# Blocks of keys handled whole: four score products, then one product with V, and the maxima tasks taken from buffers of their own

## The chip, the cores and the metric

The kernel runs on one core of one Trainium2 chip. The metric is the device time of one execution in microseconds, lower is better. The core has five engines with a queue each: PE (matrix products, from SBUF into PSUM), DVE (vector), ACT (scalar, exponentials), POOL and SP, which issues most of the DMAs here. PSUM has eight banks of 128 x 512 float32. PEld stands for the loading of PE's weights.

## The reference, cut to what matters

Two attentions over the same 2048 tokens (512 wide, 32 heads of 16) are mixed by a gate:

```
a = A(x): causal softmax attention inside 4 segments of 512, plus a linear-attention memory of earlier segments
b = B(x): qkv = x @ wqkv;  p = softmax(q k^T / 4) over all 2048 keys;  o = p v;  o @ wo
out = g * a + (1 - g) * b,     g = sigmoid(x . gate_w)
```

B is the larger part: 32 heads x 2048 x 2048 scores, all exponentiated.

## The kernel before, in words

**Projection stage** (lines 766 to 944). The images of q and k (float16, high and low halves) and of v are computed with products of twelve matmuls each (`qk_job`, `v_job`; line 311 and line 285) and stored in DRAM. A loop over 16 blocks `blk` does this for A with its memory, and takes jobs for B from a list `fill`. Between the jobs `spill()` issues pairs of maxima tasks.

**Rounds** (lines 1050 to 1085). A round `k` (32 of them) handles one unit of B and one of A; a unit is four heads (a quad) and 512 queries. In this text a *period* is one block `it` of 128 keys of a B unit, 16 per round, and the *A stretch* is what follows them in the round.

- In a period, `t_group` makes the scores of B transposed (keys on partitions): two groups, `n` even and odd, of two heads each. Heads 0 and 2 use rows 0 to 63 of PE, heads 1 and 3 rows 64 to 127, so that two products on different halves run side by side. The banks come from `T3` = `tb0`, `tb1`, `mb`. ACT exponentiates each bank into one of two buffers `PTILE`.
- `pv` multiplies the exponentials of the period before with V, four heads on four column strips, into the bank `pvb`. It is called for 256 queries after each of the two groups.
- **Maxima tasks**: the exponent of a later round needs row maxima. A task `s_b` multiplies 128 queries by 512 keys for two heads (two matmuls, line 535, into a pair of banks `sbk`) and DVE reduces the 128 x 1024 result to 128 x 2 (line 537). A unit has 32 tasks, 1024 in all. `spread` plans two per period for the next rounds' units; each stands *between* the two score products of a group (`between`), so that each of its halves runs beside one of them. `sbk` has two pairs, used in turn. The tasks read the same `QB` and `KB` buffers (three of each) as the score products.
- The A stretch has five groups of A (`t_group`, `pv`) and the six masked maxima reductions of the next A unit (`s_a`, lines 513 to 524).
- `m_chain` turns the maxima of the next units into two rows, `m_rows` puts them into the operands, `fin_copy`, `fin_load`, `fin_rec`, `fin_bc`, `fin_norm` normalise, `out_rows` (from round 9 on, a half of a 128-row block per round) multiplies by the output weights, split by rows into two banks.

The order of the work on every engine is the order in which the code is written; a queue runs in that order and waits at its head.

Of the kernel before, what the change touches and what calls it, by code (L numbers as in the profile page):

```python
# [7 lines left out]
FT = mybir.dt.float32  # L8
# [12 lines left out]
SEQ = 2048  # L21
DM = 512
C = 512
# [7 lines left out]
EARLY = 6  # L31
S_FIRST = 10
S_LAST = 10
OMI = 14
SPILLS = 64
# [3 lines left out]
def gated_mix_kernel(ctx, tc, xt, wq, wk, wv, wo, beta, wqkv, wob, gate_w, out):  # L39
# [10 lines left out]
    QB = [P.tile([128, 2, C], HF, name=f"qb{s}") for s in range(3)]  # L50
# [18 lines left out]
    KB = [P.tile([128, 2, SEQ], HF, name=f"kb{s}") for s in range(3)]  # L69
    KBF = [t.rearrange("p a t -> p (a t)").bitcast(FT).rearrange("p (k t) -> p k t", k=4) for t in KB]  # L70
# [377 lines left out]
    def load_qk(dst, kd, w, qd, c):  # L448
# [4 lines left out]
        for d0, r0, n in ((0, 0, 16), (16, 0, 32)) if w else ((0, 0, 32), (32, 16, 18)):  # L453
            for j in range(2):
                nc.sync.dma_start(dst[64 * j + d0:64 * j + d0 + n], v[qd % 2, j, r0:r0 + n, :, cs])
# [5 lines left out]
    def q_of(u):  # L461
        return QA[u % 2] if u < 32 else QB[u % 3]

    def k_of(u, p):
        return KA[u % 2][:, p] if u < 32 else KB[(u - 32) % 3][:, p]
# [9 lines left out]
    def load_kb(k, c=None):  # L475
        dst = KB[k % 3] if c is None else KB[k % 3][:, :, c * C:(c + 1) * C]
        load_qk(dst, "B", 1, k % 8, c)
# [48 lines left out]
    MXB = {}  # L526

    def s_b(u, i, p, kc):
        kd, qd, c = UN[u]
        if u not in MXB:  # L530
            MXB[u] = W.tile([128, 2, 2, 4, 4], FT, name="mxb")
        b = rot("s", SBK)
        for j in (1, 0):
            r = slice(64 * j, 64 * j + 64)
            nc.tensor.matmul(b[:, j], q_of(u)[r, p, i * 128:(i + 1) * 128],  # L535
                             k_of(u, p)[r, kc * C:(kc + 1) * C], start=True, stop=True)
        nc.vector.tensor_reduce(MXB[u][:, :, p, i, kc], b, axis=AX.X, op=OP.max)  # L537
# [3 lines left out]
    def m_chain(k):  # L541
# [3 lines left out]
        if k < 32:  # L545
            nc.vector.tensor_reduce(mx[:, 1], MXB.pop(32 + k).rearrange("q j p i c -> q (j p) i c"), axis=AX.X,
                                    op=OP.max)
        else:
            nc.vector.memset(mx[:, 1], 0.0)
# [33 lines left out]
    def t_group(u, n, banks, between=()):  # L583
# [5 lines left out]
        for it, hs in (((n // 2, (n % 2 * 2, n % 2 * 2 + 1)),) if kd == "B" else GA[n]):  # L589
# [3 lines left out]
            for j, h in enumerate(hs):  # L593
# [6 lines left out]
                PT[u, it, h] = PTILE[pn % 2][:, 2 + j if (kd, it) == ("A", 2) else h][:, c0:c0 + w]  # L600
            c0 += w
        for j in range(2):
            pt = PTILE[pn % 2][:, 2 + j if (kd, n) == ("A", 4) else hs[j]]
# [82 lines left out]
    def out_mm(c, t, a):  # L686

        b = misc()
        for n, (oi, wi, g) in enumerate([(oi, wi, g) for oi, wi in TERMS for g in range(4)]):
            nc.tensor.matmul(b, (AT["oh"], AT["ol"])[oi][:, g, a], (AT["wh"], AT["wl"])[wi][:, g, a],  # L690
                             start=n == 0, stop=n == 11)
# [7 lines left out]

    def out_rows(c, t, a, inner):  # L700
        b = [misc(), rot("s", SBK)[:, 0]]
        for n, (oi, wi, g) in enumerate([(oi, wi, g) for oi, wi in TERMS for g in range(4)]):
            for j in range(2):
                r = slice(64 * j, 64 * j + 64)
                nc.tensor.matmul(b[j], (AT["oh"], AT["ol"])[oi][r, g, a], (AT["wh"], AT["wl"])[wi][r, g, a],  # L705
                                 start=n == 0, stop=n == 11)
            if n == 2:
                for f in inner:
                    f()
                rot("s", SBK)  # L710
        if a == 0:
            AT["y"] = [AT["L"].tile([128, DM], FT, name=n) for n in ("yo", "yp")]
            nc.scalar.activation(AT["y"][0], b[0], AF.Copy)
            nc.vector.tensor_copy(AT["y"][1], b[1])
        else:
            tt = 4 * c + t
            y0, y1 = AT["y"]
            y2 = AT["L"].tile([128, DM], FT, name="yq")
            nc.scalar.activation(y2, b[0], AF.Copy)
            nc.vector.tensor_tensor(y1, b[1], y1, op=OP.add)  # L720
            nc.gpsimd.tensor_tensor(y0, y0, y2, op=OP.add)
            nc.gpsimd.tensor_tensor(y0, y0, y1, op=OP.add)
            nc.sync.dma_start(outr[tt * 128:(tt + 1) * 128, :], y0)
# [36 lines left out]
    ST_B = [(i, p, kc) for i in range(4) for p in range(2) for kc in range(4)]  # L760
    ST_A = [(0, None), (2, 0), (2, 1), (3, 0), (3, 1), (1, None)]

    def s_tasks(u):
        return [todo(s_a, u, *t) for t in ST_A] if u < 32 else [todo(s_b, u, *t) for t in ST_B]
# [21 lines left out]
    ax = [todo(set_aux, t[:, p], int(n < 3)) for n, t in enumerate(QB + KB[:1]) for p in range(2)]  # L786
    ax = [todo(set_steps, t[:, p], a) for a, ts in enumerate((KA, QA)) for t in ts for p in range(2)] + ax
    for tt in range(NT):
# [29 lines left out]
        if ax:  # L818
            ax.pop(0)()
    for n in range(8):  # L820
        w, c = divmod(n, 4)
        qk_job(0, "B", 0, w, c)
        if n < 4:
            split_wv(n)
# [8 lines left out]
    first = s_tasks(32) + s_tasks(0)  # L833
    st33 = [todo(s_b, 33, *t) for t in sorted(ST_B, key=lambda t: t[2])]
    early = st33[:EARLY]
# [7 lines left out]
    def spill():  # L843
        nonlocal quota
        quota += rate
        if quota >= 2:
            quota -= 2
            for _ in range(2):
                (first or early).pop(0)()

    S0 = [b[:, 0] for b in SBK]
    CUM = (2, 4, 6, 9, 11, 13, 16, 18, 20, 22, 24, 27, 29, 32, 34, 36)
    for blk in range(16):
        g, c = divmod(blk, 4)
        pg, pc = divmod(blk - 1, 4)
        if blk == 4:
            mode["misc"] = TB + [MB, PVB]
        rate = len(ST_A + ST_B) / SPILLS if 4 <= blk < 14 else 0
        if blk == 14:
            for p in range(2):  # L860
                set_aux(KB[1][:, p], 0, nc.sync)
            load_kb(1, 0)
# [9 lines left out]
        if blk == 2:  # L872
# [13 lines left out]
        if blk == 4:  # L886
            load_q(33)
# [19 lines left out]
        for n in range(3):  # L907
            for f in mt[n]:
                f()
            if blk == 14 and n == 2:  # L910
                quota = EARLY
# [4 lines left out]
            if blk == 14:  # L916
                load_kb(1, 1 + n)
            if nf == 35:
                mode["misc"] = [MB, PVB, TB[1]]
# [11 lines left out]
        if blk == 13:  # L931
            for f in first:
                f()
            first, quota = [], 0
        if 0 < c < NC4 - 1:
            mem_upd(g, c)
        if blk == 14:
            spill()
        if blk == 15:
            for f in early:  # L940
                f()
# [3 lines left out]


    def late():
# [9 lines left out]
        for p in range(2):  # L957
            set_aux(KB[2][:, p], 0)
# [4 lines left out]
    NG = 2 * NT + 5  # L963

    def pvs(k, n):

        ua, ub = k, 32 + k
        if n == 0:
            if k:
                pv(ua - 1, 2)  # L970
                fin_copy(ua - 1)
        elif k == 31 and n < 2 * NT:
            if n % 2 and n > 1:
                pv(ub, n // 2 - 1)
        elif 2 <= n < 2 * NT + 2:
            pv(ub, n // 2 - 1, n % 2 * 256, n % 2 * 256 + 256)
            if n == 2 * NT + 1:
                fin_copy(ub)
        elif n > 2 * NT + 1:
            m = n - 2 * NT - 2  # L980
            if m < 2:
                pv(ua, 0, 256 * m, 256 * m + 256)
            else:
                pv(ua, 1)
                pv(ua, 3)

    def extras(k):

        pre, post = {}, {}
        if not k:  # L990
            for n in range(4):
                pre[2 * n] = [fill[n - 4]]
        post[2 * S_LAST + 4] = [todo(m_rows, k + 1)]
        for n, at in [(k - 9, 1)] + [(23, 2 * OMI)] * (k == 31):
            if n >= 0:
                rows = (n // 8, n // 2 % 4, n % 2)
                pre[at] = [todo(out_rows, *rows, plan.pop((k, at))) if k < 31 else todo(out_mm, *rows)]
        return pre, post

    def beside(k, it):  # L1000

        for f, it0, u in ((fin_load, NT + 1, 32 + k), (fin_rec, 5, 31 + k), (fin_bc, 6, 31 + k),
                          (fin_load, 1, k - 1), (fin_rec, 6, k - 1), (fin_bc, S_LAST + 2, k - 1)):
# [30 lines left out]
    plan = {}  # L1034

    def spread(tasks, gs):
        for n, p in enumerate(gs):
            plan.setdefault(p, []).extend(tasks[len(tasks) * n // len(gs):len(tasks) * (n + 1) // len(gs)])

    for k in range(31):  # L1040
        if k:
            spread([todo(s_b, 33 + k, *t) for t in (sorted(ST_B, key=lambda t: t[2]) if k == 1 else ST_B)],
                   [(k - 1, n) for n in range(2 * S_FIRST, 2 * NT)] + [(k, n) for n in range(2 * S_LAST)])
        else:
            spread(st33[EARLY:], sorted([(0, n) for n in range(2 * S_LAST)] + [(0, 2 * n) for n in range(4)]))
        for n, t in enumerate(ST_A):
            plan.setdefault((k, 2 * NT + n - (n > 2)), []).append(todo(s_a, k + 1, *t))

    ex = [extras(k) for k in range(32)]
    for k in range(32):  # L1050
        ua, ub = k, 32 + k
# [89 lines left out]
```

## Time and profile before

| what | value |
|---|---|
| median of 3 runs | 1846.73 us (1845.93 to 1847.3) |
| profiled execution | 1849.68 us, span 1848.0 us, granted clock 0.997 |
| PE busy | 1807.7 us, 98% of the span |
| DVE busy | 1591.2 us, 86% |
| ACT busy | 1432.4 us, 78% |
| POOL busy | 339.3 us, 18% |
| DMA | 158.92 MB, mean 86 GB/s |

The profiled execution is 3 us above the median. A row of the timeline gives the start, the duration, the engine, the line, the operation and the operands; rows of one kind that follow each other are merged (x8). Matmuls are pipelined, so the distance between starts says how long one holds the engine, and its duration how long it takes to be done. On PE a float32 product with V shows as two records.

### The profile page before, as it was taken

How to read it: one execution, taken by the hardware profiler on the slowest of the kernel's cores; microseconds unless marked ns; L12 is line 12 of the kernel's file. 1: busy time of each engine (PE TensorE's matmuls, PEld its weight loads, DVE VectorE, ACT ScalarE, POOL GpSimd, SP SyncE). 2: the span in 40 equal slices, each digit the busy share in tenths (PEclk: the TensorE clock that was granted, in tenths of full speed). 3: DMA queues.
4: the chain of work that ended last, by engine and by line, in shares of the span. 5: the costliest groups of instructions: out<-in, count | busy, mean ns of one | idle time of the engine just before them, and what ended most of it. 6: DMA issues, size and time to landing. Idle time of an engine off the chain costs nothing.

```text
span 1848.0 us, 44286 instructions
## 1 busy us (share of the span) xinstructions
PE 1807.7 (98%) x17781; PEld 730.0 (40%) x17781; DVE 1591.2 (86%) x1772; ACT 1432.4 (78%) x2709; POOL 339.3 (18%) x691
## 2 busy tenths in 40 slices
PE   8999999899999999999999999999999999999998
PEld 6677777532222222333333333333333333333325
DVE  6334786699999999999999999999999999999942
ACT  4233333388989999989898989898989898989894
POOL 6100000101212010212121212121212121212122
PEclk9999999999999999999999999999999999999999
DMA  7554534332323222323232323232323232323111
GB/s 229 92 141 141 148 99 106 87 96 68 97 74 93 61 80 64 79 68 85 67 85 67 85 68 85 67 86 67 85 68 85 67 85 69 87 69 87 47 39 61
DMA packets 162482, 158.92 MB, mean 86 GB/s; under 512 B 40140, under 2 KB 126620, under 8 KB 162276
## 3 DMA queue, kind: packets, MB, share of 16 engines
q1 hardware_dynamic: 158692, 149.29, 29.1%
q0 software_dynamic: 3296, 6.27, 1.8%
q8 instruction: 140, 2.29, 0.5%
q14 instruction: 66, 0.54, 0.1%
q10 hardware_dynamic: 288, 0.52, 0.1%
HBM read 103.38 MB, written 50.86 MB: 83 GB/s over the span
## 4 chain that ended last, share of the span: by engine, by line
PE 80%; DVE 13%; ACT 4%; issue 2%; DMA 1%; SPq 0%; ACTq 0%; DVEq 0%; POOLq 0%
PE pvb L620 29%; PE tb L598 12%; DVE mxb L537 10%; PE sbk L535 10%; PE mb L598 6%; PE tb L311 3%; ACT raw L604 3%; PE pvb L311 2%; PE tb L705 2%; PE tb L285 2%; PE sbk L513 2%; PE sbk L285 2%; PE mb L705 1%; PE mb L311 1%; PE sbk L311 1%
## 5 line engine op out<-in xcount | busy, mean ns | idle before, releaser
L537 DVE TENSOR_REDUCE mxb<-sbk 128x2 f32<-128x1024 f32 x1024 | 1173.7, 1221 | 24.7 <-PE sbk L535 13.1
L604 ACT ACTIVATE raw<-tb 128x512 f32<-128x512 f32 x1557 | 884.5, 600 | 64.5 <-PE tb L598 30.9
L620 PE MATMUL pvb<-raw,vb 128*17 128x256 f32 (+1 forms) x8072 | 645.2, 388 | 0.0
L535 PE MATMUL sbk<-kb,qb 64*128 64x512 f16 x2048 | 552.8, 378 | 9.3 <-DVE mxb L537 8.3
L604 ACT ACTIVATE raw<-mb 128x512 f32<-128x512 f32 x780 | 468.2, 600 | 31.5 <-PE mb L598 14.4
L598 PE MATMUL tb<-qb,kb 64*128 64x512 f16 x1343 | 467.0, 381 | 1.2 <-ACT raw L604 0.8
L598 PEld LDWEIGHTS <-kb 64*128 64x128 f16 x2048 | 143.6, 93 | 414.4 <-issue 409.3
L620 PEld LDWEIGHTS pvb<-raw,vb 128*17 128x17 f32 x8072 | 138.0, 95 | 403.3 <-issue 393.8
L598 PE MATMUL mb<-qb,kb 64*128 64x512 f16 x678 | 258.2, 381 | 1.1 <-DVE st L326 1.0
L607 POOL TENSOR_SCALAR_AFFINE_SELECT raw<-raw 128x256 f32<-128x256 f32 (+1 forms) x320 | 115.3, 361 | 326.6 <-ACT raw L604 318.3
L535 PEld LDWEIGHTS <-qb 64*128 64x128 f16 x2048 | 137.3, 93 | 43.4 <-issue 33.5
L521 DVE TENSOR_REDUCE mx<-sbk 128x2 f32<-128x1024 f32 (+1 forms) x128 | 133.9, 1088 | 7.0 <-PE sbk L517 5.9
L620 PE MATMUL pvb<-raw,va 128*17 128x256 f32 (+2 forms) x1280 | 103.2, 383 | 3.8 <-ACT pvs L629 1.1
L664 POOL TENSOR_TENSOR o<-o,d 128x512 f32<-128x512 f32 x31 | 39.5, 1274 | 216.5 <-DMA d<-rd 175.9
L523 DVE TENSOR_REDUCE mx<-sbk 128x4 f32<-128x512 f32 x64 | 61.3, 958 | 12.4 <-PE sbk L517 12.4
L513 PE MATMUL sbk<-ka,qa 64*128 64x512 f16 (+3 forms) x512 | 70.5, 296 | 0.0
L598 PE MATMUL tb<-qa,ka 64*128 64x384 f16 (+3 forms) x340 | 61.7, 303 | 0.0
L652 POOL TENSOR_TENSOR rec<-rec,grow 128x16 f32<-128x16 f32 x24 | 5.3, 221 | 275.9 <-DVE rec L644 275.9
L323 ACT ACTIVATE st<-tb,rng 128x512 f16<-128x512 f32 x21 | 14.4, 687 | 53.0 <-PE tb L311 19.8
L517 PE MATMUL sbk<-cmask,crows 64*128 64x64 bf16 x1024 | 52.7, 189 | 0.0
L517 PEld LDWEIGHTS <-crows 64*128 64x128 bf16 x1024 | 46.4, 94 | 13.7
L445 POOL TENSOR_TENSOR mst<-mtmp,mst 128x136 f32<-128x136 f32 x8 | 3.6, 452 | 257.8 <-DVE mtmp L444 257.8
(330 smaller groups left out, 1732.1 us busy)
## 6 DMA issues: line engine op xcount, KB each, us to landing
vb<-vdB SPq DMA_DIRECT2D x16, 1088.0 KB
pd<-pvs SPq DMA_DIRECT2D x64, 256.0 KB
kb<-dB SPq DMA_DIRECT2D x60, 256.0 KB
dB<-st SPq DMA_DIRECT2D x64, 128.0 KB
dA<-st SPq DMA_DIRECT2D x64, 128.0 KB
o<-pd SPq DMA_DIRECT2D x64, 128.0 KB
d<-rd SPq DMA_DIRECT2D x63, 128.0 KB
kb<-dB SPq DMA_DIRECT2D x60, 128.0 KB
```

The costliest lines, as they stand in the source:

```text
L285: nc.tensor.matmul(b, (XH, XL)[xi][c][:, n % 4, tl * 128:(tl + 1) * 128], WV[wi][:, n % 4, :], start=n == 0, stop=n == 11)
L311: nc.tensor.matmul(b, WS[ws][w][wi][:, k, :], (XH, XL)[xi][c][:, k, :], start=n == 0, stop=n == 11)
L513: nc.tensor.matmul(b[:, j, c0:c0 + n], q_of(u)[r, p, i * 128:(i + 1) * 128], k_of(u, p)[r, :n], start=True, stop=False)
L517: nc.tensor.matmul(b[:, j, c0 + n - 128 + w.start:c0 + n - 128 + w.stop], crows[r, n2 - 1], cmask[r, n2 - 1, w], start=False, stop=n2 == 2)
L521: nc.vector.tensor_reduce(m[:, :, p, i], b[:, :, :n], axis=AX.X, op=OP.max)
L523: nc.vector.tensor_reduce(m[:, :, :, i], b.rearrange("q j (p k) -> q j p k", p=2)[:, :, :, :n], axis=AX.X, op=OP.max)
L535: nc.tensor.matmul(b[:, j], q_of(u)[r, p, i * 128:(i + 1) * 128], k_of(u, p)[r, kc * C:(kc + 1) * C], start=True, stop=True)
L537: nc.vector.tensor_reduce(MXB[u][:, :, p, i, kc], b, axis=AX.X, op=OP.max)
L598: nc.tensor.matmul(bs[j][:, c0:c0 + w], k_of(u, h // 2)[r, 128 * it:128 * it + 128], q_of(u)[r, h // 2, q0:], start=True, stop=True)
L604: nc.scalar.activation(pt, bs[j], AF.Exp, scale=AT["esc", kd, qd // 2])
L607: nc.gpsimd.affine_select(out=m, in_=m, pattern=[[1, 128]] if n < 2 else [[0, 2], [1, 128]], compare_op=OP.is_ge, fill=0.0, base=0, channe ...
L620: nc.tensor.matmul(PVB[32 * h:32 * h + E + 1, q0 + lo:q0 + hi], vt[:, it, 4 * q + h, :], pt[:, lo:hi], start=it == 0 and lo == 0, stop=it ...
```

## The change

In words:

- A period issues all four score products of a block of keys, into four banks `ET` = `tb0`, `tb1` and the two halves of the *second* pair `sbk1`; then one product with V over all 512 queries (`b_group`, `pv`). The order of the heads alternates with the half task (below).
- A period carries one and a half maxima tasks instead of two: a full one in the *first* pair `sbk0`, and one half of a second task in the bank `mb`, whose other half goes into the next period (`half_task`). In the A stretch some five more full tasks stand (`extra`).
- The tasks have operand buffers of their own (`QM`, `KM`, two each, loaded by `fetch`) and take units in the order `ORD`; their results lie in eight places of `MXB`. `AHEAD` = 160 tasks (before: 32, and six of the next unit) are issued in the projection stage, in pairs after the jobs from block 2 on, before round 0.
- `out_rows` is gone; `out_mm` makes a whole product into `mb` in the A stretch, with one task inside. `QB` and `KB` have two buffers instead of three, and SP loads them at period 2 of the round before.

```diff
-EARLY = 6
-S_FIRST = 10
-S_LAST = 10
-OMI = 14
-SPILLS = 64
+AHEAD = 160
+SPILLS = 96
+CHAIN_AT = 10
+ROWS_AT = 12
...
-    QB = [P.tile([128, 2, C], HF, name=f"qb{s}") for s in range(3)]
+    QB = [P.tile([128, 2, C], HF, name=f"qb{s}") for s in range(2)]
+    QM = [P.tile([128, 2, C], HF, name=f"qm{s}") for s in range(2)]
+    MXB = P.tile([128, 8, 2, 2, 4, 4], FT, name="mxb")
...
-    KB = [P.tile([128, 2, SEQ], HF, name=f"kb{s}") for s in range(3)]
+    KB = [P.tile([128, 2, SEQ], HF, name=f"kb{s}") for s in range(2)]
+    KM = [P.tile([128, 2, SEQ], HF, name=f"km{s}") for s in range(2)]
...
+    ORD = [0, 8, 1, 9, 2, 3, 4, 5, 6, 7] + list(range(10, 32))
+    TASKS = [(n, i, p, kc) for n in range(32) for i in range(4) for p in range(2) for kc in range(4)]
...
+    def s_red(b, t, js):
+        n, i, p, kc = t
+        m = MXB[:, place[n][1], :, p, i, kc]
+        if len(js) == 2:
+            nc.vector.tensor_reduce(m, b, axis=AX.X, op=OP.max)
+        else:
+            nc.vector.tensor_reduce(m[:, js[0]:js[0] + 1], b, axis=AX.X, op=OP.max)
+        if (i, p, kc) == (0, 1, 0):
+            fetch(n + 1)
...
-    first = s_tasks(32) + s_tasks(0)
+    first = [s_b] * 32 + s_tasks(0) + [s_b] * (AHEAD - 32)
...
-        rate = len(ST_A + ST_B) / SPILLS if 4 <= blk < 14 else 0
+        rate = len(first) / (SPILLS - hold["spills"]) if blk > 1 else 0
...
+    ET = TB + [SBK[1][:, j] for j in range(2)]
+    def b_group(u, it, full, half):
...
+        j = half[1] if half else 1
+        hs = (1 - j, 3 - j, j, 2 + j)
+        for n, h in enumerate(hs):
+            k_mm(h)
+            if n == 0 and half:
+                s_mm(MB, half[0], j)
+            if n == 2 and full:
+                for jj in (1 - j, j):
+                    s_mm(SBK[0][:, jj], full, jj)
+        if half:
+            s_red(MB, half[0], (j,))
+        if full:
+            s_red(SBK[0], full, (0, 1))
+        for h in hs:
+            PT[u, it, h] = pt = PTILE[(it + u) % 2][:, h]
+            nc.scalar.activation(pt, ET[h], AF.Exp, scale=AT["esc", kd, qd // 2])
...
     for k in range(32):
         ua, ub = k, 32 + k
+        rows = [(n // 8, n // 2 % 4, n % 2) for n in range(k - 9, k - 8) if n >= 0]
+        for it in range(NT):
+            busy = it == ROWS_AT
+            b_group(ub, it, next_task() if hold["next"] < 1024 else None,
+                    half_task() if not busy and (hold["half"] or hold["next"] < 1024) else None)
...
+            if it:
+                pv(ub, it - 1)
...
+        for n in range(5):
+            t_group(ua, n, banks)
...
+            if hold["half"]:
+                t, j = half_task()
+                s_mm(MB, t, j)
+                s_red(MB, t, (j,))
+            for _ in range((1, 1, 0, 1, 1 + (k % 4 == 3))[n]):
+                extra()
+            if n == 1 and k < 31:
+                for r in rows:
+                    out_mm(*r, extra)
+                if not rows:
+                    extra()
```

PE's queue before, one group of a period, two of which make the period (`sbk_120` and `sbk_121` are the two pairs, `raw` the exponentials, LDWEIGHTS the weight loads):

```order
L598 LDWEIGHTS kb_91
L598 MATMUL mb<-qb_69,kb_91 128x512
L535 LDWEIGHTS qb_70
L535 MATMUL sbk_120<-kb_89,qb_70 128x512
L535 LDWEIGHTS qb_70
L535 MATMUL sbk_120<-kb_89,qb_70 128x512
L598 LDWEIGHTS kb_91
L598 MATMUL tb_116<-qb_69,kb_91 128x512
L620 MATMUL pvb<-raw_86,vb_75 17x256 x4
L598 LDWEIGHTS kb_91
```

PE's queue now, one period inside a round (`sbk_124` is the second pair, which here holds scores; `sbk_123` and `mb` hold tasks):

```order
L971 MATMUL tb_119<-qb_68,kb_91 128x512
L553 LDWEIGHTS qm_71
L553 MATMUL mb<-km_94,qm_71 128x512
L971 LDWEIGHTS kb_91
L971 MATMUL sbk_124<-qb_68,kb_91 128x512
L971 LDWEIGHTS kb_91
L971 MATMUL tb_120<-qb_68,kb_91 128x512
L553 LDWEIGHTS qm_71
L553 MATMUL sbk_123<-km_94,qm_71 128x512
L553 LDWEIGHTS qm_71
L553 MATMUL sbk_123<-km_94,qm_71 128x512
L971 LDWEIGHTS kb_91
```

Behind these rows the fourth score product follows, again into `sbk_124`, and then the whole product with V. Two of a period's four score products now share the pair `sbk_124`, in second and fourth place.

DVE's queue before, around an A stretch (the last tasks of a round, the six reductions of the next A unit, the next tasks):

```order
L537 TENSOR_REDUCE mxb<-sbk_121 128x2
L523 TENSOR_REDUCE mx<-sbk_120 128x4
L521 TENSOR_REDUCE mx<-sbk_121 128x2
L521 TENSOR_REDUCE mx<-sbk_120 128x2
L521 TENSOR_REDUCE mx<-sbk_121 128x2
L521 TENSOR_REDUCE mx<-sbk_120 128x2
L523 TENSOR_REDUCE mx<-sbk_121 128x4
L537 TENSOR_REDUCE mxb<-sbk_120 128x2
```

and now, at the same place of a round below 9:

```order
L524 TENSOR_REDUCE mx<-sbk_124 128x4
L562 TENSOR_REDUCE mxb<-mb 128x1
L560 TENSOR_REDUCE mxb<-sbk_123 128x2
L522 TENSOR_REDUCE mx<-sbk_124 128x2
L560 TENSOR_REDUCE mxb<-sbk_123 128x2
L560 TENSOR_REDUCE mxb<-sbk_124 128x2
L522 TENSOR_REDUCE mx<-sbk_123 128x2
L522 TENSOR_REDUCE mx<-sbk_124 128x2
L522 TENSOR_REDUCE mx<-sbk_123 128x2
L560 TENSOR_REDUCE mxb<-sbk_124 128x2
L524 TENSOR_REDUCE mx<-sbk_123 128x4
L560 TENSOR_REDUCE mxb<-sbk_124 128x2
```

Five full tasks and a half one now stand among the six reductions of A, where none stood.

More of the change, by code (lines that the diff above doesn't have):

```diff
@@ L944, in gated_mix_kernel @@
             load_vb(0)
+    for n in range(4):
+        if n == 3:
+            mode["misc"] = [MB, PVB, TB[1]]
+        fill[nf + n]()
+        spill()
+    for f in first:
+        f()
     def late():
```

270 lines of the change are left out of this document (112 added, 158 removed).

## The prediction

> **What bounds the kernel now.** I read the page first, then the busy times by stage, then the timeline of one period. The page's slices show three engines that are all nearly full from slice 8 on:
>
> ```profile
> PE   8999999899999999999999999999999999999998
> ...
> DVE  6334786699999999999999999999999999999942
> ACT  4233333388989999989898989898989898989894
> ...
> PEclk9999999999999999999999999999999999999999
> ```
>
> The stretches (start:end, length, busy of PE, PEld, DVE, ACT, POOL, granted clock, DMA share) give the projection stage, rounds 1 to 8, rounds 9 to 30, and the last round with the tail. The row with one engine is DVE's time for the maxima tasks in the projection stage:
>
> ```profile
> 120.00:346.00 226.00, 220.78 (x1128) 167.77 (x1128) 149.74 (x259) 77.07 (x159) 15.87 (x26) 1.00 0.46 128
> ...
> 411.00:771.00 360.00, 354.40 (x3936) 103.74 (x3935) 353.42 (x369) 325.63 (x609) 56.31 (x115) 1.00 0.29 78
> 771.00:1777.00 1006.00, 1001.77 (x11332) 322.57 (x11328) 952.63 (x935) 902.87 (x1706) 211.86 (x441) 1.00 0.28 75
> 1777.00:1848.00 71.00, 65.95 (x401) 30.19 (x392) 21.86 (x52) 42.25 (x88) 13.90 (x26) 1.00 0.16 52
> ...
> 120.00:346.00 226.00, 44.84 (x39) 1.00 0.46 128
> ```
>
> In rounds 1 to 8 DVE is busy 98%, so DVE sets the pace; from round 9 on PE (99.6%) does. The copies at the ends of A units give the length of a round: 30 rounds between 412.9 and 1778.9, 45.5 us each. In a period both engines meet:
>
> ```profile
> L627 DVE COPY pvs<-pvb x31: 680/681/691, 412.9 to 1778.9; 128x512 f32<-128x512 f32 x31
> ...
> 599.61 9.14 DVE L537 TENSOR_REDUCE mxb<-sbk 128x2 f32<-128x1024 f32 x8
> ...
> 605.35 0.39 PE L598 MATMUL tb<-qb,kb 64*128 64x512 f16 x1
> 605.40 0.55 PE L535 MATMUL sbk<-kb,qb 64*128 64x512 f16 x2
> 605.62 0.37 PE L598 MATMUL tb<-qb,kb 64*128 64x512 f16 x1
> 605.92 0.63 PE L620 MATMUL pvb<-raw,vb 128*17 128x256 f32 x8
> 606.48 0.39 PE L598 MATMUL mb<-qb,kb 64*128 64x512 f16 x1
> ...
> 631.70 0.39 PE L598 MATMUL tb<-qa,ka 64*128 64x512 f16 x2
> ...
> 638.64 0.39 PE L598 MATMUL tb<-qb,kb 64*128 64x512 f16 x1
> ```
>
> Eight reductions take 9.14 with the last one's 1.22: one per 1.131 us. A group lasts from 605.35 to 606.48, 1.13 as well, so a period of two groups and two tasks takes 2.26. The A stretch takes 6.94 (631.70 to 638.64). Inside a group four half-array products need 0.57 and the half product with V 0.56.
>
> **What the new period costs.** The waits in the new program decide it. Both halves of the second pair of banks belong to one tile, and the program treats it as a whole: the period's second exponential (of the second product, in that pair) waits for the *fourth* product, which writes the pair's other half; and the next period's second product waits for this period's *fourth* exponential, since that reads the pair. In 451 of 480 steps between periods this wait is written out; in the other 29 a wait that comes no earlier stands ahead of it. So a ring runs through every period: second product, fourth product, second, third, fourth exponential, next second product. Its links were all seen before, where nothing else held them:
>
> ```profile
> 351.19 1.08 ACT L604 ACTIVATE raw<-tb 128x512 f32<-128x512 f32 x2 [3.73 <-PE mb L311]
> 351.84 0.37 PE L598 MATMUL tb<-qb,kb 64*128 64x512 f16 x1 [0.76 <-ACT raw L604]
> ...
> 353.69 0.37 PE L598 MATMUL mb<-qb,kb 64*128 64x512 f16 x1 [0.99 <-DVE st L326]
> ...
> 354.10 0.60 ACT L604 ACTIVATE raw<-mb 128x512 f32<-128x512 f32 x1 [0.27 <-PE mb L598]
> ```
>
> - Second to fourth product: between them stand the third and the task's two halves; on the fourth's half of PE two products come first. In a group the fourth starts 0.27 after the first with one ahead of it (605.35 to 605.62), so one costs about 0.21 and two 0.43.
> - Product to exponential: 353.69 to 354.10, 0.41; I take 0.45, because the second exponential has a wait of its own ahead of it in ACT's queue.
> - Two exponentials in 1.08 with 0.60 for the last: 0.48 from start to start; from the second to the fourth 0.97.
> - Exponential to the product that waits for its bank: 351.19 to 351.84, 0.65.
>
> Sum 2.50 us; I use 2.49. Bounds: 2.43 with the smallest values, 2.55 with the largest.
>
> PE itself would need less. Whole products with V stand in round 31:
>
> ```profile
> 1790.42 1.22 PE L620 MATMUL pvb<-raw,vb 128*17 128x512 f32 x8
> ...
> 1792.38 1.04 PE L620 MATMUL pvb<-raw,vb 128*17 128x512 f32 x7
> ...
> 1804.33 0.37 PE L598 MATMUL tb<-qb,kb 64*128 64x512 f16 x1
> 1804.63 1.05 PE L620 MATMUL pvb<-raw,vb 128*17 128x512 f32 x8
> ...
> 1805.61 0.39 PE L598 MATMUL tb<-qb,kb 64*128 64x512 f16 x1
> ```
>
> Last score product to V 0.30, whole product 0.98 (two halves took 1.12, so one change of shape is saved), three slots of 0.21 from first to fourth: 1.93. So PE would wait 0.56 in each period for the fourth exponential. DVE has 1.13 and a half task: the nearest reduction of 512 columns takes 0.70 (row below), 0.61 from start to start by the same 0.09 that the full one is shorter: 1.74. All three engines idle in the ring, and a period does 1.5 tasks in 2.49 us where it did 2 in 2.26.
>
> `m_rows` (period 12) now has `mb` alone, and the half task behind it waits for ACT's copy of the rows: 0.2 a round.
>
> **The A stretch.** A round still needs 32 tasks; 16 full, 16 halves and 5.25 more make 29.25. The 5.25 stand among the six reductions of A, for which I use these rows:
>
> ```profile
> L521 DVE TENSOR_REDUCE mx<-sbk 128x2 f32<-128x768 f32 x64 | 61.4, 959 | 7.0 <-PE sbk L517 5.9
> ...
> L523 DVE TENSOR_REDUCE mx<-sbk 128x4 f32<-128x512 f32 x32 | 22.3, 698 | 12.4 <-PE sbk L517 12.4
> ```
>
> DVE there: 5.25 x 1.13 + 3 x 1.13 + 2 x 0.87 + two of 0.61 = 12.3 us, where PE had 6.94 and gets 5.25 x 0.3 on top. With two pairs of banks PE can run only two reductions ahead, so DVE becomes the bound of this stretch. It can't begin early: the first scores of A go into the second pair, free with the last fourth exponential (0.8 after the stretch begins), and DVE starts 1.25 after the begin. From the last period's second product to the begin: 0.43 + 0.30 + 0.98 = 1.71. To the next round's second product, which needs the pair that the last task holds: 1.71 + 1.25 + 12.3 = 15.3. A round below 9: 15 x 2.49 + 0.2 + 15.3 = 52.9.
>
> From round 9 on `out_mm` puts twelve whole matmuls into one bank (3.06, below), where `out_rows` stood beside tasks in a period; DVE has one task to do meanwhile and runs dry for about a microsecond, and adds 0.7 every other round: 54.3. Entirely hidden it would be 52.9, entirely in the open 56.
>
> ```profile
> 1807.78 3.06 PE mb L690 x12
> ```
>
> **The projection stage** gets 160 tasks where it had 38 (and the masked six). For PE a pair costs 0.53 (227.78 to 228.31):
>
> ```profile
> 227.50 0.69 ACT L323 ACTIVATE st<-mb,rng 128x512 f16<-128x512 f32 x1 [2.10 <-PE mb L311]
> ...
> 227.78 0.61 PE L535 MATMUL sbk<-kb,qb 64*128 64x512 f16 x4
> ...
> 228.22 0.75 DVE L326 SCALAR_TENSOR_TENSOR st<-mb,rng,st 128x512 f16<-128x512 f32 x1 [2.04 <-ACT st L323]
> ...
> 228.31 2.13 PE L311 MATMUL tb<-xh,ws 128*128 128x512 f32 x8
> ...
> 346.48 0.39 PE L598 MATMUL tb<-qb,kb 64*128 64x512 f16 x1
> ```
>
> so 122 more are 33 us: the lower bound. DVE's share: 149.7 - 44.8 = 105 us of other work from 120 to 346 (block 2 on), plus 160 x 1.13 and the six: 292 in a stretch of 226 + 12 (the four v jobs that stood in round 0). That is 54 too much. On top DVE waits at each job's result for ACT's part (0.7 from 227.50 to 228.22, say 0.6 for sixty jobs), and PE, with both pairs of banks in DVE's queue, stops until they are reduced: 90. I take 85, between 33 and 105. Round 0 begins at 346.5 + 12 + 85 = 444.
>
> **What is free.** SP gets 218 more DMAs, eight a round for the tasks' operands; they are issued a unit (some 45 us) ahead, DMA engines are 28% busy, and nobody waits. The loads of `QB` and `KB` move from two rounds to one round ahead, still 40 us. POOL loses two additions a round; it is idle most of the time.
>
> **Sum.** 444 + 9 x 52.9 + 20 x 54.3 = 2006 to round 29, where the tasks run out (864 in the rounds / 29.25 = 29.5). Without a task the ring has one slot less, 2.27: round 29 about 49, round 30 46; the last round and tail 71 + 16 x (2.27 - 1.96, the step between the two V products above) = 76. Together 2177, with the 1.7 outside the span 2179, against 1849.7 of the profiled run; the median stood 3 lower, so 2175. DVE's busy time hardly changes, so its share falls to some 74%.
>
> **Rivals.**
> - *The ring is not closed, and nothing waits for the tasks* (the change does what it says): a period then takes what ACT needs, 1.96 as in round 31; 16 x 1.96 + A on PE's own 8.6, with the output 11.6: 40.2 and 43.2 a round; the projection pays PE's 33 alone: 392 + 9 x 40.2 + 20 x 43.2 + 42 + 40 + 71 = 1771, *faster* by 4%. It decides only if DVE's backlog in A and in the projection stays under two tasks; the 12.3 against 8.6 speaks against it. 0.03.
> - *The ring is shorter*: the exponentials go by their own products, the fourth still frees the second product's bank. PE's 1.71 from second to next first product, and 0.41 + 3 x 0.49 + 0.65 from first to next second make 2 T = 4.24, T = 2.12: 15 x 0.37 x 29.5 = 164 less, 2010. 0.07.
> - *PE's clock falls.* It did so here after a wait of 1.59 us (end of the row at 439.30 to 441.28):
>
> ```profile
> 439.30 0.39 PE L598 MATMUL tb<-qb,kb 64*128 64x512 f16 x1
> 441.28 0.54 PE L535 MATMUL sbk<-kb,qb 64*128 64x512 f16 x2 [1.59 <-DVE mxb L537]
> ...
> 443.54 0.60 PE L598 MATMUL tb<-qb,kb 64*128 64x512 f16 x1
> ...
> 445.19 0.39 PE L598 MATMUL tb<-qb,kb 64*128 64x512 f16 x1
> ...
> 400.00:450.00 50.00, 48.18 (x520) 13.61 (x516) 48.09 (x50) 43.00 (x82) 7.32 (x14) 0.97 0.24 68
> ```
>
>  A group took 1.65 instead of 1.13 (443.54 to 445.19), then the speed was back. At that speed the ring's PE links double: 0.43 more and 0.2 for a product's slower end, 3.1 a period. If every other stretch were slow: 0.3 x 452 = 140 more, 2315. Here it takes a wait of 1.5 us at once or in two pieces; the new period's is 0.56, two in 3.4 us 1.1. 0.08.
>  The Trainium skill, "TensorE: Matmul & The Clock Gate", section "A second HAM failure mode: psum-queue depth-cycling", says that PE's short idling between groups, as it cycles through PSUM banks, can make the clock go to and fro, which would give the 2315; its Part 1 says that the clock falls after a wholly idle window of about 3.4 us, by which it would never fall here. This trace stands between: one wait of 1.59 us sufficed.
>
> **How the numbers follow.** The likeliest case, ring and DVE-bound A stretches, has 0.81, with 2090 to 2245 of its own (512 periods x 0.06 = 30 either way, A 29 x 0.7 = 20, projection -50 to +20). The range reaches toward the shorter ring and the falling clock: 2050 to 2250; it leaves out the rest of the 0.18 of the rivals. Faster by over 0.2% (about what a measurement of this kernel can tell from none): 0.03, the first rival. Within 0.2%: 0.01, something between. Slower: 0.96.
>
> **What would show it.** Right: periods of 2.45 to 2.55 with PE's wait for the exponential of line 989 before a score product, some 0.5 in each, the largest wait on PE; DVE without gaps in A stretches of about 13 us and with gaps in periods; first score product of round 0 near 444; rounds of 53 to 54; the last two shorter. Wrong: periods near 2.0, or A stretches near 8. A granted clock under 0.95 in the rounds would speak for the third rival.

## The result and the profile after

| | before | after |
|---|---|---|
| median (lowest to highest) | 1846.33 us (1845.85 to 1847.3) | 2273.73 us (2270.84 to 2278.26) |
| ratio after / before, 95% interval | | 1.232 [1.229, 1.234] |
| profiled execution, its span | 1849.7, 1848.0 us | 2271.7, 2269.9 us |
| PE, DVE, ACT busy | 1807.7, 1591.2, 1432.4 us | 1902.3, 1673.6, 1427.3 us |
| first score product of round 0 | 346.48 us | 488.86 us |

The changed kernel is slower by 23%. The direction and the ring that the prediction described held, its term for the projection stage did not; the time lies 24 us above the range's upper end.

The page's slices, after. No engine is full any more from slice 8 on, and the clock has an 8 in two early slices:

```profile
PE   8988878788888888888888888888888888888888
...
DVE  6377877778787887787777777777777777877421
ACT  3222212247777777777777777777777777777884
...
PEclk9999989899999999999999999999999999999999
```

The stretches after (columns as before). The first two are the projection stage, the third rounds 0 to 8, the last rounds 9 to 28:

```profile
120.00:346.00 226.00, 181.86 (x872) 122.13 (x871) 176.59 (x237) 50.62 (x103) 9.68 (x15) 0.93 0.32 92
346.00:412.00 66.00, 56.05 (x245) 38.22 (x245) 53.61 (x77) 14.27 (x29) 0.45 (x1) 0.90 0.37 94
...
489.00:983.00 494.00, 406.24 (x3214) 113.76 (x3217) 395.65 (x461) 362.89 (x685) 60.09 (x125) 0.97 0.32 81
983.00:2094.00 1111.00, 940.90 (x7414) 289.33 (x7410) 871.76 (x956) 819.12 (x1541) 166.78 (x380) 1.00 0.32 78
```

In rounds 9 to 28 PE is busy 85%, DVE 78%, ACT 74%: all three wait in turn. One period in the timeline shows for whom (PE's four score products are lines 971, ACT's exponentials line 989):

```profile
1221.45 0.37 PE L971 MATMUL tb<-qb,kb 64*128 64x512 f16 x1 [0.26 <-ACT raw L989]
...
1221.94 0.37 PE L971 MATMUL sbk<-qb,kb 64*128 64x512 f16 x1
...
1222.38 0.38 PE L971 MATMUL sbk<-qb,kb 64*128 64x512 f16 x1
...
1222.86 0.60 ACT L989 ACTIVATE raw<-sbk 128x512 f32<-128x512 f32 x1 [0.41 <-PE sbk L971]
1223.36 0.59 ACT L989 ACTIVATE raw<-tb 128x512 f32<-128x512 f32 x1
...
1223.83 0.60 ACT L989 ACTIVATE raw<-sbk 128x512 f32<-128x512 f32 x1
...
1224.49 0.37 PE L971 MATMUL sbk<-qb,kb 64*128 64x512 f16 x1
```

This is the ring of the prediction, link by link: second product at 1221.94, fourth at 1222.38, the *second* exponential (of the bank written at 1221.94) only at 1222.86, the third and the fourth at 1223.36 and 1223.83, the next second product at 1224.49. Medians over all periods: 0.448 + 0.478 + 0.970 + 0.657 = 2.553 us, and the median period is 2.553.

The list of waits sums these up (us in total, times, longest):

```profile
DVE mxb L562 <- PE mb L553: 242.0, 381, 1.3
ACT raw L989 <- PE sbk L971: 220.4, 507, 0.8
PE tb L971 <- ACT raw L989: 120.3, 415, 1.2
PE sbk L553 <- DVE mxb L560: 102.4, 143, 3.3
```

ACT's 220 us stand in 507 of 512 periods. PE's largest wait is for the exponential; the last row is PE waiting for task reductions. The prediction's sign was one wait of some 0.5 us on PE in each period. It came in two pieces: 0.26 of idle time before the first product, and a second product that starts 0.49 after the first (1221.45 to 1221.94), where one slot is 0.21. From 120 to 489 us, the projection stage with tasks, that wait and DVE's own for ACT are

```profile
PE sbk L553 <- DVE mxb L560: 64.5, 71, 3.3
...
DVE st L328 <- ACT st L325: 47.0, 41, 2.9
...
120.00:489.00 369.00, 301.69 (x1419) 202.18 (x1417) 288.80 (x384) 81.78 (x164) 13.33 (x22) 0.93 0.32 88
```

with DVE busy 288.8 of 369 us. There a pair of tasks waits, and then PE is slow for some microseconds:

```profile
224.42 2.35 DVE L560 TENSOR_REDUCE mxb<-sbk 128x2 f32<-128x1024 f32 x2
225.69 0.61 PE L553 MATMUL sbk<-km,qm 64*128 64x512 f16 x2 [2.31 <-DVE mxb L560]
...
226.82 0.61 PE L553 MATMUL sbk<-km,qm 64*128 64x512 f16 x2 [0.52 <-DVE mxb L560]
227.35 3.78 PE L287 MATMUL tb<-wv,xh 128*128 128x512 f32 x8
...
233.41 2.11 PE L287 MATMUL pvb<-wv,xh 128*128 128x512 f32 x8
...
224.60:231.30 6.70, 5.10 (x13) 3.34 (x13) 6.54 (x10) 0.00 (x0) 0.00 (x0) 0.50 0.13 36
```

Eight matmuls of one shape took 3.78 us after a wait of 2.31, and 2.11 six microseconds later. The last row gives the granted clock between: 0.50.

### The profile page after: what moved, and what is told of

Same layout as the page of the kernel before. It is cut to its first block, busy times and chain, and to the rows that moved or that the text cites. A ratio compares the mean times of both kernels' runs of the same rounds, so it can differ in the third digit from the quotient of the medians.

```text
span 2269.9 us, 36207 instructions
## 1 busy us (share of the span) xinstructions
PE 1902.3 (84%) x13537; PEld 742.6 (33%) x13537; DVE 1673.6 (74%) x1994; ACT 1427.3 (63%) x2697; POOL 318.8 (14%) x681
## 5 line engine op out<-in xcount | busy, mean ns | idle before, releaser
L560 DVE TENSOR_REDUCE mxb<-sbk 128x2 f32<-128x1024 f32 x787 | 952.6, 1222 | 61.2 <-PE sbk L553 59.5
L989 ACT ACTIVATE raw<-sbk 128x512 f32<-128x512 f32 x1024 | 615.6, 601 | 220.8 <-PE sbk L971 220.4
L989 ACT ACTIVATE raw<-tb 128x512 f32<-128x512 f32 x1024 | 609.5, 595 | 55.1 <-PE mb L553 48.2
L657 PE MATMUL pvb<-raw,vb 128*17 128x512 f32 x4096 | 539.7, 599 | 0.0
L562 DVE TENSOR_REDUCE mxb<-mb 128x1 f32<-128x512 f32 x474 | 327.2, 690 | 242.5 <-PE mb L553 242.0
L971 PE MATMUL sbk<-qb,kb 64*128 64x512 f16 x1024 | 379.0, 376 | 65.5 <-ACT raw L989 14.7
L553 PE MATMUL sbk<-km,qm 64*128 64x512 f16 x1574 | 317.9, 382 | 127.1 <-DVE mxb L560 102.4
L553 PEld LDWEIGHTS <-qm 64*128 64x128 f16 x2048 | 135.9, 94 | 299.7 <-issue 292.6
L553 PE MATMUL mb<-km,qm 64*128 64x512 f16 x474 | 183.0, 386 | 10.6 <-ACT mr L607 10.6
L641 ACT ACTIVATE raw<-tb 128x512 f32<-128x512 f32 x221 | 125.3, 600 | 99.1 <-PE tb L635 72.4
L641 ACT ACTIVATE raw<-mb 128x512 f32<-128x512 f32 x95 | 56.5, 595 | 11.5 <-PE tb L635 10.1
```

Of the source, the lines that this page charges most:

```text
L553: nc.tensor.matmul(b, QM[n % 2][r, p, i * 128:(i + 1) * 128], KM[place[n][0]][r, p, kc * C:(kc + 1) * C], start=True, stop=True)
L560: nc.vector.tensor_reduce(m, b, axis=AX.X, op=OP.max)
L562: nc.vector.tensor_reduce(m[:, js[0]:js[0] + 1], b, axis=AX.X, op=OP.max)
L641: nc.scalar.activation(pt, bs[j], AF.Exp, scale=AT["esc", kd, qd // 2])
L657: nc.tensor.matmul(PVB[32 * h:32 * h + E + 1, q0 + lo:q0 + hi], vt[:, it, 4 * q + h, :], pt[:, lo:hi], start=it == 0 and lo == 0, stop=it ...
L971: nc.tensor.matmul(ET[h], k_of(u, h // 2)[r, 128 * it:128 * it + 128], q_of(u)[r, h // 2, :], start=True, stop=True)
```

## The experiments

### Which banks are one tile

The changed kernel, with the place of the pair in the period moved.

```diff
-    ET = TB + [SBK[1][:, j] for j in range(2)]
+    ET = [TB[0], SBK[1][:, 0], SBK[1][:, 1], TB[1]]
...
-            nc.tensor.matmul(ET[h], k_of(u, h // 2)[r, 128 * it:128 * it + 128], q_of(u)[r, h // 2, :],
+            nc.tensor.matmul(ET[n], k_of(u, h // 2)[r, 128 * it:128 * it + 128], q_of(u)[r, h // 2, :],
...
-            nc.scalar.activation(pt, ET[h], AF.Exp, scale=AT["esc", kd, qd // 2])
+            nc.scalar.activation(pt, ET[n], AF.Exp, scale=AT["esc", kd, qd // 2])
```

Here `n` is the position in the period; before, the order of heads put the pair at positions 2 and 4. `ET[n]` also gives each position one fixed bank, where the changed kernel swaps the two single banks, and the two halves of the pair, from period to period.

> The changed kernel, with one thing different: which bank each score product of a period writes. The pair of banks that is one tile holds products 2 and 3 instead of 2 and 4 (products 1 and 4 get the two single banks). Theory (the ring through the pair sets the period): the second exponential now waits for the third product and the next second product for the third exponential, so the ring is 0.2 + 0.45 + 0.48 + 0.66 = 1.8 us and no longer binds; PE and ACT need 1.93 each. Period 1.95 to 2.05 us where the changed kernel has 2.55; 480 x 0.5 to 0.6 less, so 1985 to 2035 us; PE's wait for the exponential (120 us) nearly gone; projection stage and A stretches unchanged. Rival 1 (the period is long for another reason: DVE's tasks, the clock, the whole V product in one piece): period stays at 2.45 or more, 2230 or more. Rival 2 (DVE cannot keep up once periods are 2.0): period 2.2 to 2.3, about 2130.

Measured: 2026.31 us (2017.89 to 2027.22), ratio to before 1.096 [1.094, 1.098]; 247 us less than the changed kernel. Median period 1.953. One period and a stretch of three:

```profile
1121.85 0.39 PE L971 MATMUL tb<-qb,kb 64*128 64x512 f16 x1
...
1122.08 0.38 PE L971 MATMUL sbk<-qb,kb 64*128 64x512 f16 x2
...
1122.77 1.10 ACT L989 ACTIVATE raw<-sbk 128x512 f32<-128x512 f32 x2
1122.82 1.05 PE L657 MATMUL pvb<-raw,vb 128*17 128x512 f32 x8
...
1123.80 0.39 PE L971 MATMUL tb<-qb,kb 64*128 64x512 f16 x1
...
1120.00:1126.00 6.00, 6.00 (x49) 1.86 (x48) 5.74 (x8) 6.00 (x13) 0.22 (x1) 1.00 0.92 182
```

PE and ACT are both busy 6.00 of 6.00 us: the period is at the bound that the prediction put at 1.93 for PE alone. The theory stands, both rivals fall.

> The changed kernel, with the pair of banks under products 1 and 4. Ring theory: first product to fourth 0.49 + 0.45, fourth to first exponential 0.48, first to fourth exponential 3 x 0.485, fourth exponential to the next first product 0.66: 3.5 us a period, so 480 x 0.97 = 465 more, about 2740 us. Rival (the period does not hang on which products share the pair): 2.55 and 2270 as before.

Measured: 2612.1 us in one run, 338 more than the changed kernel; median period 3.258. The sign and the mechanism are the theory's, the size is smaller than expected. The rows name the link:

```profile
1222.16 0.37 PE L971 MATMUL sbk<-qb,kb 64*128 64x512 f16 x1 [1.24 <-ACT raw L989]
...
1222.83 0.38 PE L971 MATMUL sbk<-qb,kb 64*128 64x512 f16 x1
...
1223.31 0.60 ACT L989 ACTIVATE raw<-sbk 128x512 f32<-128x512 f32 x1 [1.19 <-PE sbk L971]
...
1224.76 0.62 ACT L989 ACTIVATE raw<-sbk 128x512 f32<-128x512 f32 x1
...
1225.42 0.37 PE L971 MATMUL sbk<-qb,kb 64*128 64x512 f16 x1 [1.24 <-ACT raw L989]
```

First to fourth product takes 0.67, not 0.94: the second product no longer waits for anything of its own, so three slots lie between. 0.67 + 0.48 + 1.45 + 0.66 = 3.26, the measured period.

> The changed kernel, with products 1 and 2 in the pair of banks. Ring theory: the second product comes 0.2 to 0.5 after the first, first exponential 0.43 to 0.48 after that, second exponential 0.48 later, and the next first product 0.66 after it: 1.8 to 2.1 us, against PE's and ACT's 1.95. Period 1.95 to 2.15, between the pair at 2 and 3 (1.95) and the changed kernel (2.55), nearer the former: 2025 to 2085 us. Rival (any place but 2 and 3 closes the long ring): 2.4 or more, 2200 or more.

Measured: 2070.1 us in one run, median period 2.084, as expected. So the same four banks give periods of 1.95, 2.08, 2.55 or 3.26 us, by which two of them the program takes for one. The three new places have fixed banks and the 2.55 has swapped ones; a pair at 2 and 4 with fixed banks was not run, nor one with the two halves as tiles of their own. That the ring and not the swap makes the 2.55 rests on its links, whose measured sum is the whole period.

### The projection stage

```diff
-            nc.vector.tensor_reduce(m, b, axis=AX.X, op=OP.max)
+            nc.vector.tensor_reduce(m, b[:, :, :hold["cols"]], axis=AX.X, op=OP.max)
```

with `cols` 64 until the stage ends and 512 after it: the kernel leaves out seven eighths of each reduction there.

> The changed kernel, but in the projection stage a maxima task's reduction reads 64 of each 512 columns (its result is not used rightly; the rest of the work is unchanged). Theory (DVE's backlog of reductions stops PE, and the falling clock follows from these stops): PE's wait for the reductions before round 0 (64.5 us) falls under 10, the granted clock between 120 and 400 us is 0.98 or more, and the first score product of round 0 comes at 395 to 415 (358.7 where the kernel before would have had it, 33 for the pairs of products, about 10 for the rest) instead of 489; the whole time falls by 75 to 95, to about 2185. Rival 1 (the loss is in the order: each projection job waits for ACT and DVE, whatever the reductions take): PE's waits fall by half at most, 440 to 455. Rival 2 (the clock falls by itself when small products alternate with projection jobs): clock stays at 0.90 to 0.93, 425 to 440 with PE's waits gone.

Measured: 2191.52 us in one run, 82 less; round 0 begins at 411.74:

```profile
411.74 0.38 PE L973 MATMUL tb<-qb,kb 64*128 64x512 f16 x1
...
120.00:346.00 226.00, 211.74 (x1105) 144.23 (x1103) 117.76 (x309) 65.08 (x132) 10.15 (x16) 0.99 0.42 118
346.00:412.00 66.00, 62.52 (x318) 41.95 (x316) 27.32 (x75) 16.82 (x32) 3.21 (x6) 1.00 0.33 86
...
PE sbk L553 <- DVE mxb L560: 14.9, 17, 1.5
```

The clock is 0.99 to 1.00 with the same products on PE, and PE's wait for the reductions up to 412 us is 14.9 us (under 10 was expected). The theory stands: 77 of the stage's 130 us (488.9 against 358.7, which is the 346.5 of before and the 12 of the four v jobs) hang on what the reductions take on DVE, the clock's fall among them; 53 is left with short reductions: the 33 that the prediction counted for the pairs on PE, the wait of 15, and 5 more.

How much of the 77 is DVE's work, and how much its order:

```diff
-        if quota >= 2:
-            quota -= 2
-            for _ in range(2):
-                if first:
-                    first.pop(0)()
+        while quota >= 1:
+            quota -= 1
+            if first:
+                first.pop(0)()
```

and a `spill()` also between the sixth and the seventh matmul of each `v_job` and `qk_job`, with `SPILLS` 159 instead of 96. So two things change together: how many tasks are issued at a time, and where.

> The changed kernel, with the same 160 tasks (and the six reductions for unit A) in the projection stage issued one at a time, after a job and also between its sixth and seventh matmul (160 places), instead of two at a time at 96 places less often. DVE's total work and the rounds are the same. Theory (most of the loss in this stage is order: a pair takes both pairs of banks, so PE stops until both reductions are through DVE's queue, and then the clock falls): PE's wait for the reductions between 120 and 489 us falls from 64.5 to below 25, the granted clock there rises from 0.93 to 0.97 or more, the first score product of round 0 comes at 425 to 450 instead of 489; about 2215 to 2235 us in all. Rival (DVE's total work decides: 289 us of work and its in-order waits, wherever a task stands): waits of 50 or more, first product at 475 or later, 2260 or more.

Measured: 2245.35 us in one run, 28 less. PE's wait for the reductions between 120 and 489 us halves, to the row below, the clock there is 0.96, round 0 begins at 460.94:

```profile
PE sbk L557 <- DVE mxb L564: 31.0, 36, 1.9
...
460.94 0.39 PE L975 MATMUL tb<-qb,kb 64*128 64x512 f16 x1
```

This lies between the two expectations. The edit was worth 28 of the 77 us here. The stage moves by some 8 us from run to run: it ended at 496.7 with the pair at 2 and 3, with the same program up to there as the 488.9. With the pair at 2 and 3 the same edit moves that end from 496.7 to 453.6, 43 us.

The granted clock tells these runs apart. It was 0.93 and 0.90 up to the 488.9 and the 496.7, and 0.96 and 0.99 up to the 460.9 and the 453.6. One minus the clock, times the length from 120 us on, gives the clock time lost: 26, 38, 14 and 3 us. Between two runs of the same program up to there, 12 us more of it go with 7.9 us more of the stage, and 10 with 7.3, though PE's waits for the reductions are alike (64.5 and 63.3 us up to 489; 31.0 and 31.2). By this estimate one lost microsecond costs about 0.7: the clock has some 18 of the changed kernel's 130 us, and the edit without the clock is worth about 19 in both pairs of runs.

> Both edits together: products 2 and 3 of a period in the pair of banks, and the projection stage's tasks one at a time. Theory: the two gains lie in different stages and add: 2026 less what the other kernel gains against 2274 (40 to 60), so 1965 to 1985 us. Rival (a stage that ends earlier is paid back by the first rounds): 2010 or more.

Measured: 1989.22 us (1984.13 to 1997.85), ratio 1.078 [1.074, 1.081]: 37 less than with the banks alone, a little less than the 40 expected at least. The gains add, within the scatter of the projection stage.

Then 132 tasks ahead instead of 160, on top of both edits (`AHEAD = 132`):

> The kernel with both edits (products 2 and 3 in the pair of banks, projection tasks one at a time), with 132 tasks ahead instead of 160; the 28 others run in rounds 29 and 30, which had none. Theory (in the projection stage a task still costs about what DVE takes for it, since DVE is busy 86% and PE waits for it there): 28 x 0.7 to 1.13 = 20 to 32 off the projection stage (first score product at 422 to 437 instead of 454), rounds 29 and 30 longer by 5 to 7 together (46.8 as the others, instead of 43.1 and 42.6); 15 to 25 less in all: 1965 to 1975 us. Rival (one at a time, the tasks are hidden and cost PE's 0.27 each): 8 off the projection stage, nothing or 2 in all: 1987 or more.

Measured: 1968.36 us (1965.24 to 1970.51), ratio 1.066 [1.065, 1.068]. Round 0 begins at 429.76, where it was 453.64:

```profile
429.76 0.39 PE L975 MATMUL tb<-qb,kb 64*128 64x512 f16 x1
```

24 us for 28 tasks, 0.85 each, much nearer to DVE's 1.13 than to PE's 0.27; the clock in this stage is 0.99 in both runs, so it hardly touches the comparison. So a further task in the projection stage costs nearer DVE's time than PE's. This is the fastest version with the changed period, and still 6.6% slower than the kernel before.

### The A stretch

The five tasks a round that stand in the A stretch have their reductions cut to 64 columns, by the same `cols`.

> The changed kernel, but the 5.25 tasks that stand in each A stretch have their reduction read 64 of each 512 columns (their maxima are not used rightly; PE's part is kept). Theory (DVE's 12.3 us of reductions set the A stretch): they cost DVE 1.0 less each, 5.2 a round; PE and ACT then set it, as in rounds 29 and 30, which have no tasks (10.8 and 11.0 from the last exponential of B to the first of the next B), plus 5.25 x 0.3 of products less the output in the rounds below 9: A stretches of 9.5 to 12 us where the changed kernel has 12.5 to 16; 2.5 to 3.5 less a round, so 2170 to 2200 us. Rival (PE's own work and the output's twelve matmuls set the stretch): under 1 us a round, 2245 or more.

Measured: 2207.67 us in one run, 66 less. Two A stretches (rounds 4 and 10) of this kernel:

```profile
738.00:748.00 10.00, 8.37 (x116) 3.56 (x115) 7.73 (x12) 6.08 (x12) 3.60 (x10) 1.00 0.13 42
1046.00:1059.00 13.00, 11.94 (x131) 5.86 (x133) 8.42 (x14) 7.22 (x14) 4.83 (x11) 1.00 0.15 52
```

and the same two of the changed kernel:

```profile
753.00:765.50 12.50, 9.09 (x116) 3.81 (x116) 11.50 (x12) 6.16 (x12) 3.61 (x10) 1.00 0.10 33
1080.00:1094.00 14.00, 12.16 (x131) 5.94 (x130) 12.33 (x14) 7.39 (x14) 5.56 (x13) 1.00 0.14 49
```

Below round 9 DVE is 92% busy, and the stretch falls from 13.8 to 10.7 us on average (last exponential of B to the first of the next B): DVE sets it. From round 9 on it falls only from 14.6 to 13.6: with the output's matmuls PE has 12 of those 13 us itself, 92%. Whole rounds, by their first score products, fall by 3.5 us (rounds 0 to 8) and by 1.6 (9 to 28), which makes 64 of the 66. The theory holds for the first nine rounds; in the other twenty DVE and PE bind nearly together, which the expectation missed, and so the time lies above its 2170 to 2200.

### The whole product with V alone

The kernel before, with one edit:

```diff
-        elif k == 31 and n < 2 * NT:
+        elif n < 2 * NT:
```

> The kernel before, with one part of the change alone: one whole product with V after a period's second group instead of a half after each group; tasks, order and banks as before. Theory: PE saves 0.13 us a period (0.98 for a whole against 1.12 for two halves), 2.1 a round. Rounds 9 to 30 (PE full) go from 45.7 to DVE's 45.0, rounds 1 to 8 (DVE full) stay: 15 us less, 1831. Rival: with three banks for score products, the fourth now follows 0.84 us after the first and waits for the first exponential (0.41 + 0.65 = 1.06 after it); 0.2 a period on PE, which takes the saving and more: period 2.32, about 1870.

Measured: 1904.63 us (1904.45 to 1906.92), ratio 1.032 [1.030, 1.033]. The rival holds, larger than it said. One period:

```profile
999.97 0.39 PE L598 MATMUL tb<-qb,kb 64*128 64x512 f16 x1
...
1000.39 0.60 ACT L604 ACTIVATE raw<-tb 128x512 f32<-128x512 f32 x1 [0.30 <-PE sbk L535]
...
1001.04 0.37 PE L598 MATMUL tb<-qb,kb 64*128 64x512 f16 x1
...
1002.33 0.39 PE L598 MATMUL mb<-qb,kb 64*128 64x512 f16 x1
```

The fourth product waits for the first exponential, 0.65 after its start: three banks do not carry four products in a row. The period is 2.36 against 2.26. So the half products with V of the kernel before fit its three banks, and a whole product wants a fourth one, which the change takes from the tasks; no run gives the kernel before a fourth bank.

## Why the prediction was right and where it was wrong

The sum, with the step of each part (span, us; the first score products of rounds 0, 9 and 29 come at 488.9, 983.3 and 2094.4):

| part | predicted | measured | difference |
|---|---|---|---|
| begin of round 0 | 444 | 488.9 | +45 |
| rounds 0 to 8 | 9 x 52.9 = 476 | 494.4 | +18 |
| rounds 9 to 28 | 20 x 54.3 = 1086 | 1111.1 | +25 |
| round 29 to the end | 171 | 175.5 | +4 |

- **The ring: right.** Same links, same order, shown by moving the pair to three other places. It is 0.063 longer than 2.49 (product to exponential 0.478 where 0.45 was taken, second to fourth product 0.448 for 0.43, bank to product 0.657 for 0.65): 30 us over 480 steps. The upper bound of 2.55 was the value. PE's own need of 1.93, whose terms add to 1.91, shows as 1.95 once the pair stands at 2 and 3.
- **The wait for the maxima's rows: mis-sized.** From first exponential to first exponential, periods 12 and 13 are 0.06 and 0.29 longer than the median, where 0.2 was taken for both, and the first period is 0.16 longer, for which nothing was taken: 0.5 a round, 9 us more in all.
- **The A stretch: right in size, half right in cause.** From the last period's second product to the next round's it takes 15.6 us on average in rounds 0 to 8, where 15.3 was predicted, and 16.6 in rounds 9 to 28, where 15.3 + 1.4 was. Rounds were 1.3 to 2.0 us longer than predicted, and ring and rows account for 0.063 x 15 + 0.3 = 1.25 of that. Below round 9 most of the rest is the 0.3 by which the stretch itself is longer and, once, round 0's second product, which starts 3.2 us after the first. From round 9 on PE with the output binds as nearly as DVE.
- **The projection stage: the step that failed.** The term of 85 us measured 130, above even its upper bound of 105. The prediction filled DVE's queue without gaps (292 us of work) and added PE's stops. But DVE was busy only 289 of the 369 us from 120 to 489: its reductions stand in order behind operations that wait for ACT (47 us in this stretch), PE then stops (64.5 us), and its clock falls, 0.93 in the mean, so the next job comes later to DVE too. A bound worked out from a full engine is none when the two engines stop each other in turn. Of the 130 us, 53 remain when the reductions are short. By the estimate above some 18 are the clock's and 19 go with the pairs and their places; the other 40 or so hang on DVE's reductions wherever they stand. The last three are an estimate, not a measurement.
- **The rival of the falling clock** came, in another place than the prediction priced it: in the projection stage, where waits of over 2 us stand, and little in the rounds (0.97 up to round 8, then 1.00). Up to round 8 it fell once at the begin of round 0 and seven times in A stretches (rounds 1, 2, 3, 6 and 7). Five of the seven come where PE waits for reductions four times in a row, 0.5 to 0.7 us each, the other two behind the waits that end a stretch. The last two of the four waits in round 1, and the clock behind them:

```profile
592.52 0.34 PE L514 MATMUL sbk<-ka,qa 64*128 64x384 f16 x2 [0.52 <-DVE mxb L560]
...
593.65 0.61 PE L514 MATMUL sbk<-ka,qa 64*128 64x512 f16 x2 [0.73 <-DVE mxb L560]
...
593.20:596.50 3.30, 2.85 (x26) 1.06 (x25) 2.46 (x4) 0.57 (x2) 0.41 (x1) 0.50 0.16 39
```

  In such an A stretch PE is idle for up to 2.0 us within 3.4 us, from round 9 on, where the output's matmuls stand between, for at most 1.4. The waits in the periods (0.26 us before the first product, 0.1 before the second in the timeline above) left it at 1.00 from round 9 on. So the psum-queue cycling of the Trainium skill ("TensorE: Matmul & The Clock Gate", section "A second HAM failure mode: psum-queue depth-cycling") does not show in the periods of this trace.
- **The range** already added the upper ends of all three errors: 30 for the ring, 20 for the A stretch and 20 for the projection stage make its 2245. The ring used its 30 and the rest of the rounds 13. The projection stage took 45 where 20 was allowed, 25 too many, and the time lies 24 beyond the range: by this count that term alone carried it out, by little.
- **DVE's share** came out at the predicted 74% by luck: its busy time, which was hardly to change, rose by 82 us, and the span was longer than predicted too.
- The *ring not closed* rival fell, and with it the change's case: even with the ring open (1.953 a period) the rounds take 47.3 us, below round 9 and above, against 45.0 and 45.7 before. The reading is that four banks for products leave the tasks one pair and a half, so that DVE's work is pushed into the A stretch and the projection stage; the runs with short reductions show what it costs there (66 and 82 us), not that it could not be placed otherwise.

## What to carry to other kernels

Ask of every bank which other bank the program counts as the same tile: a product late in the period that writes the second half closes a ring through everything between, and here the position of the two halves alone was worth 1.95 to 3.26 us a period. When work is moved to a stage that has room on average, look at the order in the engine's queue and at the buffers that it holds: DVE at 78% stopped PE for 64 us. And a lone saving of PE time (the whole product with V) is none if it bunches the products that need banks: it cost 58 us here.

## What the runs showed of the hardware that was not expected

- The granted clock follows short waits. It was 0.50 from 224.6 to 231.3 us, with a wait of 2.31 us that ends at 225.69, and eight matmuls took 3.78 instead of 2.11 us. The Trainium skill ("TensorE: Matmul & The Clock Gate", Part 1) has the clock fall after an idle window of about 3.4 us; the trace has it after less. In the changed kernel's trace it falls 19 times before the end. These falls begin whole multiples of 3.41 us apart and last 3.41 or 6.83 us. By the starts and ends of PE's rows, the 3.41 us ahead of each hold 1.24 to 3.02 us of idle time. Behind the first 20 us, no stretch of that grid at full clock with more than 1.67 us of idle time went without a fall.
- A late transfer can reach PE through POOL's queue. Where rounds are shorter, single rounds are 3 to 4 us longer than their neighbours. One of them in the kernel with both edits:

```profile
1045.94 1.26 POOL L705 TENSOR_TENSOR o<-o,d 128x512 f32<-128x512 f32 x1 [10.42 <-DMA d<-rd]
...
1047.30 0.29 POOL L596 TENSOR_SCALAR mx<-mx 128x32 f32<-128x32 f32 x1
...
1048.19 0.85 PE L609 MATMUL mb<-ident,m 128*32 128x128 f32 x4 [2.11 <-POOL m L598]
```

  POOL's normalisation waits for its transfer, the four small operations of the maxima behind it wait too, and PE for them; that period took 5.11 us, where the median of its place in the round is 2.14. The prediction had called POOL idle and said of the transfers that nobody waits for them.
